# Units of 256 tokens of one batch instead of 128 tokens of two batches, with the state carried inside the unit

## The chip, the cores and the metric

One core of one Trainium2 chip runs the whole program. The metric is device time in microseconds (us). A kernel is run several times, beside runs of the kernel before on the same chip. Each run comes with the mean clock that was granted to TensorE, as a share of full speed. Runs marked slow are left out of every ratio. Stretches of a trace are counted from the start of the profiled execution. Its span is about 2 us shorter than the device time, so spans are compared with spans and times with times.

## The reference, cut to what matters

```python
# q, k, v, alpha: (batch 4, heads 8, tokens 768, width 48), float32
for t in range(S):                       # gated linear attention
    state = alpha[:, :, t, :, None] * state + einsum('bhd,bhe->bhde', k[:, :, t], v[:, :, t])
    y[:, :, t] = einsum('bhd,bhde->bhe', q[:, :, t], state)
x = y.transpose(0, 2, 1, 3).reshape(B * S, H * D)       # 3072 x 384
g = maximum(x @ w1, x @ w2)                              # 384 -> 1024
return g @ w_out                                         # 3072 x 384
```

Both kernels use max(a, b) = relu(a - b) + b. The hidden layer is relu(x (w1 - w2)), and the rest is x (w2 w_out), with w2 w_out computed once at the start. The recurrence is done in chunks of 128 tokens. A chunk needs the scores of its tokens (q k, masked), what they take from the state before it, and the new state, which is k v summed plus the old state times its decay.

## The kernel before

A unit is one chunk of 128 tokens of two batches, so its two halves are independent. There are 12 units. Unit u takes its state from unit u - 2, and units 0 and 1 take none. Loads go out on SP's queue and outputs on ScalarE's. All matmuls are float16.

```python
def load_alpha(u):                    # two halves, rows of two tokens (384 B)
    ...
    for bb in range(2):
        nc.sync.dma_start(out=t["af"][64 * bb : 64 * bb + 64], in_=alpha[...])
def load_kqv(u, bbs):                 # rows of one token (192 B), 128 partitions
    ...
    for name, src in (("kf", k), ("qf", q), ("vf", v)):
        nc.sync.dma_start(out=t[name][:, lo:hi]..., in_=src[2 * g + lo : 2 * g + hi, :, c * C : (c + 1) * C, :]...)
...
def state(u):                         # GpSimd: old state times decay, both batches at once
    if u >= NG:
        ...
        nc.gpsimd.tensor_mul(out=X["sb"], in0=st[u - NG]["tm"], in1=dd...)
...
for u in range(2, NU):                # the loop, cut
    pairs(u, 0)                       # scores (pp) of half 0, two masks (pt) on VectorE
    kv(u)                             # k v sums; VectorE adds sb -> tm
    ...                               # hidden groups 0, 1 of unit u - 1; decays, k, state of u + 1
    pairs(u, 1)
    hid(u - 1, 2); ystate(u); hid(u - 1, 3)
    ...; yin(u)                       # ya += masked scores times v
    outp(u - 1, 0); ...; xturn(u); ...; outp(u - 1, 1)   # ends with the store, on ScalarE's queue
    load(u + 4)
```

"Dummies" are matmuls on zeros that keep TensorE busy in the start-up while it waits.

## Time and profile before

| | before |
|---|---|
| time, 4 runs beside the changed kernel | 154.81 us median (154.14 to 155.47) |
| span of the profiled run, mean granted clock | 152.9 us, 0.997 |
| first hidden matmul of unit 0 | 25.36 us |
| hidden layer of unit 1 starts | 41.76 us |
| unit 2, unit 3, unit 11 start (first score matmuls) | 45.36, 53.51, 134.47 us |
| last output copy ends | 150.19 us |

These times come from the timeline of TensorE. In the groups of instructions, "idle before" is the idle time of an engine just before the instruction, with the instruction or transfer that ended it.

### The profile page before, as it was taken

What the parts mean: (1) busy time and instruction counts of PE and PEld (TensorE: products, weight loads), DVE (VectorE), ACT (ScalarE), POOL (GpSimd) and SP (SyncE); (2) the same over time, 40 slices, a digit from 0 to 9 for tenths busy, and PEclk for the clock granted to TensorE, in tenths of its full rate; (3) what the DMA queues carried; (4) which work ended last, traced back from release to release, by engine and by line L of the source; (5) the groups of instructions that cost most, each with busy time, mean ns of one, the idle gap of its engine ahead of it and who ended that gap; (6) DMA issues with size and microseconds to landing.
All of it is one profiled execution on the core that took longest, in us unless ns stands there. A gap on an engine that the chain in (4) does not pass through costs nothing.

```text
span 152.9 us, 4086 instructions
## 1 busy us (share of the span) xinstructions
PE 140.0 (92%) x1671; PEld 96.0 (63%) x1671; DVE 93.2 (61%) x192; ACT 78.5 (51%) x165; POOL 47.5 (31%) x73
## 2 busy tenths in 40 slices
PE   6878888787699999999999999999999999999991
PEld 2236454454386676777776777777767767767660
DVE  5057815676279596687685857876849565653010
ACT  3374136713566576194491861935818529244421
POOL 6032220340171816236072180450811705400000
PEclk9999999999999999999999999999999999999998
DMA  3999999999999999997999999999999992020202
GB/s 82 203 392 216 355 224 324 179 200 139 268 192 191 168 260 142 209 245 164 195 225 210 194 251 175 278 188 226 222 191 235 189 145 82 4 103 4 101 2 103
DMA packets 93459, 28.58 MB, mean 187 GB/s; under 512 B 87424, under 2 KB 93056, under 8 KB 93440
## 3 DMA queue, kind: packets, MB, share of 16 engines
q1 hardware_dynamic: 90160, 23.60, 88.3%
q10 hardware_dynamic: 3280, 4.72, 9.1%
q8 instruction: 13, 0.21, 0.7%
q14 instruction: 6, 0.05, 0.1%
HBM read 23.59 MB, written 4.72 MB: 185 GB/s over the span
## 4 chain that ended last, share of the span: by engine, by line
PE 65%; SPq 15%; DMA 9%; ACT 3%; DVE 2%; issue 1%; ACTq 1%; POOL 0%; DVEq 0%
PE op L370 19%; PE hp L352 17%; PE op L368 8%; SPq L80 7%; DMA qf<-in_q_dram 6%; PE tp L243 5%; SPq L103 4%; DMA vf<-in_v_dram 4%; PE pp L279 3%; PE cs L186 3%; PE ya L303 2%; PE kv L259 2%; SPq L68 2%; PE xp L318 2%; DVE pt L281 2%; PE ya L291 2%
## 5 line engine op out<-in xcount | busy, mean ns | idle before, releaser
L232 POOL TENSOR_TENSOR kn<-kf,Em 128x384 f16<-128x384 f32 x24 | 23.6, 1000 | 71.7 <-ACT Em L197 60.2
L352 PE MATMUL hp<-xt,w 128*128 128x256 f16 x288 | 37.6, 273 | 2.0 <-DVE w L409 1.2
L281 DVE TENSOR_TENSOR pt<-pp,u 128x512 f16<-128x512 f32 x48 | 30.9, 686 | 13.0 <-PE pp L279 12.6
L370 PE MATMUL op<-wo,gT 128*128 128x384 f16 x192 | 35.1, 326 | 0.0
L373 ACT COPY outs<-op 128x384 f32<-128x384 f32 x24 | 11.5, 478 | 41.9 <-PE op L370 41.9
L352 PEld LDWEIGHTS <-w 128*128 128x128 f16 x288 | 25.7, 98 | 7.7 <-DVE w L409 2.5
L370 PEld LDWEIGHTS <-gT 128*128 128x128 f16 x192 | 18.8, 98 | 12.4
L245 DVE COPY qk<-tp 128x1024 f16<-128x1024 f16 x24 | 16.5, 687 | 10.4 <-PE tp L243 10.3
L357 ACT ACTIVATE gT<-hp 128x512 f16<-128x512 f32 x36 | 20.4, 593 | 3.8 <-PE hp L352 3.6
L236 DVE TENSOR_TENSOR qn<-qf,cs 128x384 f16<-128x384 f32 x24 | 12.3, 548 | 9.6 <-ACT de L207 6.4
L160 ACT ACTIVATE lg<-af 128x768 f16<-128x768 f32 x12 | 10.1, 843 | 11.7 <-DMA af<-in_alpha_dram 7.5
L368 PE MATMUL op<-w2o,xt 128*128 128x384 f16 x72 | 15.6, 325 | 0.0
L359 DVE TENSOR_SCALAR gT<-hp 128x512 f16<-128x512 f32 x12 | 8.3, 691 | 8.3 <-PE hp L352 8.3
L416 PE MATMUL warm<-wz 128*128 128x512 f16 x39 | 12.2, 439 | 1.3 <-DVE halves L123 1.3
L197 ACT ACTIVATE Em<-cs 128x384 f32<-128x384 f32 x24 | 11.7, 488 | 1.1 <-PE cs L186 1.1
L169 POOL CAST v<-vf 128x768 f16<-128x768 f32 (+1 forms) x14 | 10.2, 730 | 6.1 <-DMA vf<-in_v_dram 6.1
L202 ACT ACTIVATE cs<-cs 128x384 f32<-128x384 f32 x24 | 11.8, 492 | 0.0
L267 DVE TENSOR_TENSOR tm<-kv,sb 64x192 f32<-64x192 f32 x32 | 11.3, 353 | 0.5
L243 PE MATMUL tp<-ident,qn 128*128 128x128 f16 x96 | 9.3, 219 | 1.2 <-DVE qn L236 1.2
L279 PEld LDWEIGHTS <-qk 48*128 48x128 f16 x192 | 6.2, 94 | 6.1 <-issue 3.4
L243 PE MATMUL tp<-ident,kn 128*128 128x128 f16 x96 | 9.3, 219 | 0.4 <-POOL kn L232 0.4
L279 PE MATMUL pp<-qk 48*128 48x128 f16 x192 | 9.5, 217 | 0.2 <-DVE qk L245 0.2
(57 smaller groups left out, 142.6 us busy)
## 6 DMA issues: line engine op xcount, KB each, us to landing
af<-in_alpha_dram SPq DMA_DIRECT2D x24, 192.0 KB, 5.5
out_dram<-outs ACTq DMA_DIRECT2D x11, 384.0 KB, 4.0
kf<-in_k_dram SPq DMA_DIRECT2D x10, 384.0 KB, 6.0
qf<-in_q_dram SPq DMA_DIRECT2D x10, 384.0 KB, 7.6
vf<-in_v_dram SPq DMA_DIRECT2D x10, 384.0 KB, 7.0
w2f<-in_moe_w_dram SPq DMA_DIRECT2D x3, 512.0 KB, 5.1
wof<-in_moe_w_out_dram SPq DMA_DIRECT2D x2, 768.0 KB, 7.4
w1f<-in_moe_w_dram SPq DMA_DIRECT2D x4, 384.0 KB, 8.7
```

The source lines that it names most:

```text
L202: nc.scalar.activation(out=X["csv"][bb], in_=X["csv"][bb], func=ACTF.Exp)
L232: nc.gpsimd.tensor_mul(out=X["kn"][bb][:, :, 0:D], in0=X["kf"][:, bb], in1=X["Em"][bb])
L236: nc.vector.tensor_mul(out=X["qn"][bb][:, :, 0:D], in0=X["qf"][:, bb], in1=X["csv"][bb])
L243: nc.tensor.transpose(tp[:, n, j, :], pair(src, j), ident)
L245: nc.vector.tensor_copy(out=qk, in_=tp)
L279: nc.tensor.matmul(pa[a][:, j, :], lhsT=qk[r, 1, j, :], rhs=qk[r, 0, j, :], start=True, stop=True)
L281: nc.vector.tensor_mul(out=pt[:, a], in0=pa[a], in1=u16.unsqueeze(1).to_broadcast([128, HP, C]))
L352: nc.tensor.matmul(hp[:, n, :], lhsT=w12[:, ds, f * 128 : (f + 1) * 128], rhs=X["xt"][:, ds].rearrange("p n t -> p (n t)"), start=(ds == 0 ...
L357: nc.scalar.activation(out=gT[:, 2 * f2 : 2 * f2 + 2, :], in_=hp, func=ACTF.Relu)
L368: nc.tensor.matmul(op, lhsT=X["xt"][:, ds, n, :], rhs=w2o[:, ds, :], start=(ds == 0), stop=False)
L370: nc.tensor.matmul(op, lhsT=X["gT"][:, f, n * C : (n + 1) * C], rhs=wo16[:, f, :], start=False, stop=(f == NF - 1))
L416: nc.tensor.matmul(warm, lhsT=wz[:, 0:128], rhs=wz, start=True, stop=True)
```

## The change

The intent is wider rows. Within one batch, alpha and v of 256 tokens can be loaded as 128 partitions of two tokens each. That gives one transfer for each, with rows of 384 B instead of 192 B for v. k and q are brought into the same (parity, pair) order by two transfers for each half. The price is that the second half of a unit now needs the state of its first half, in every unit from the first on.

```diff
+    def load_fat(u, name, src):                 # alpha and v: one transfer, 384 B rows
+        nc.sync.dma_start(out=t[name].rearrange("p h j d -> p h (j d)"),
+                          in_=rows(src, u, 0, 2 * C).rearrange("h (p j) d -> p h (j d)", j=2))
+    def load_rows(u, name, src, cc):            # k and q: two transfers of 64 partitions
+        for j in range(2):
+            nc.sync.dma_start(out=t[name][64 * j : 64 * j + 64, cc],
+                              in_=rows(src, u, cc * C, C).rearrange("h (p j) d -> j p h d", j=2)[j])
...
-    def state(u):                               # once a unit, from unit u - 2
+    def state(u, cc):                           # once a half
+        if cc: tm, de0 = X["tm0"], X["de"][:, :, 0, 0]           # from the first half
+        else:  tm, de0 = st[u - B]["tm1"], st[u - B]["de"][:, :, 1, 0]
...
-        nc.gpsimd.tensor_copy(out=X["v16"][:, e], in_=X["vf"][:, e])
+        for cc, j in ((0, 0), (1, 1), (0, 1), (1, 0)):           # v casts: GpSimd and ScalarE
...
-            nc.scalar.dma_start(out=dst, in_=X["outs"])
+            nc.sync.dma_start(out=dst[j], in_=X["outs"][r])       # for j in 0, 1: halves, on SP
...
     for u in range(2, NU):
-        pairs(u, 0)
-        kv(u)
+        if u + 4 < NU:
+            load(u + 4)
+        pmm(u, 0); kvmm(u, 0); pmask(u, 0); kvsum(u, 0)
+        state(u, 1)
+        if more(u): kvmm(u, 1)
```

The start-up is reordered to match: both weight products and the whole of unit 0's attention come before its first hidden matmul.

## The prediction

> **What bounds the kernel now.** I read the page's engine table and its 40 slices first.
>
> ```profile
> PE 140.0 (92%) x1671; PEld 96.0 (63%) x1671; DVE 93.2 (61%) x192; ACT 78.5 (51%) x165; POOL 47.5 (31%) x73
> ...
> PE   6878888787699999999999999999999999999991
> ...
> DMA  3999999999999999997999999999999992020202
> ```
>
> TensorE has gaps only in the first 12 slices (46 us). The DMA row is just as full up to slice 33, so the next question is which of the two sets the pace. The table by stretches of 10 us answers it.
>
> ```profile
> 0.00:10.00 10.00, 7.35 (x41) 2.96 (x42) 2.81 (x25) 4.35 (x8) 3.89 (x15) 1.00 0.88 203
> 10.00:20.00 10.00, 8.69 (x95) 4.98 (x93) 7.80 (x15) 4.19 (x6) 2.33 (x3) 1.00 1.15 293
> 20.00:30.00 10.00, 8.20 (x65) 4.76 (x63) 4.60 (x6) 6.29 (x13) 1.83 (x2) 1.00 1.12 245
> 30.00:40.00 10.00, 7.77 (x86) 4.53 (x84) 6.62 (x14) 2.46 (x5) 2.00 (x3) 1.00 1.16 194
> 40.00:50.00 10.00, 9.16 (x129) 6.73 (x127) 7.08 (x14) 6.56 (x15) 4.47 (x6) 1.00 1.26 204
> ...
> 80.00:90.00 10.00, 10.00 (x137) 7.42 (x136) 7.17 (x15) 5.73 (x14) 3.67 (x6) 1.00 1.26 215
> ```
>
> The first number after the width is TensorE's busy time. Of its 12.9 idle us (152.9 - 140.0), 8.8 lie before 50 us; afterwards TensorE is solid. So there are two stages. The **prologue** (weights, units 0 to 2) ends at 53.5 us, where unit 3's first score matmuls start. The **steady loop** follows; the chain that ended last, read in order of time, is TensorE alone there:
>
> ```profile
> 84.12 0.33 PE pp L279 x8
> 84.45 0.45 PE kv L259 x8
> 84.90 1.31 PE hp L352 x12
> ...
> 92.94 1.30 PE op L370 x8
> 94.24 0.33 PE pp L279 x8
> ```
>
> One unit takes 94.24 - 84.12 = 10.12 us, all matmuls. From 53.5 to the end are 99.4 us that no transfer can shorten.
>
> The prologue, in the timeline, is paced by weights: w1 lands in quarters, VectorE subtracts, TensorE follows.
>
> ```profile
> 24.34 1.99 DVE L409 TENSOR_TENSOR w<-w1f,w2f 128x768 f16<-128x768 f32 x2 [2.18 <-DMA w1f<-in_moe_w_dram]
> ...
> 25.36 0.83 PE L352 MATMUL hp<-xt,w 128*128 128x256 f16 x6 [0.32 <-DVE w L409]
> ```
>
> **What the Trainium skill says.** "DMA: Bandwidth & Descriptors", section Specifications, puts the least size for line rate at 512 B. The trace agrees: by windows of 1 us, stretches of 192 B rows run at 180 to 210 GB/s, alpha's 384 B rows at 280 to 330, w2's 4 KB rows at 406 to 414. Its section Rules for kernel authors says that two transfers to disjoint partition halves serialize and are better joined. The change joins alpha's halves but splits every k and q transfer into halves; no run shows yet what that costs. "GPSIMD Engine Reference", section 4.1, calls GpSimd about 2x slower on two-input work; kn takes 1000 ns there, qn of the same shape 548 ns on VectorE. "TensorE: Matmul & The Clock Gate", section Back-to-back issue gap, gives N/2.4 + 2.5 ns when warm: 162.5 ns for 384 columns. The chain's 8 in 1.30 us are 162.5: no slack inside.
>
> **The change, part by part.**
>
> *Transfers.* Before, each unit loads 1024 rows of 384 B (alpha) and 6144 of 192 B; after, 2048 of 384 B (alpha, v) and 4096 of 192 B. At 190 and 310 GB/s: 1.18 MB/190 + 0.39/310 = 7.5 us before, 0.79/190 + 0.79/310 = 6.7 after: 0.8 us less a unit. In the prologue w2 no longer waits for v of unit 0, so weights land about 0.8 to 1 us earlier. Issues per unit go from 5 to 10 at 0.6 us each, 6 us, below the 6.7: hidden. In the loop the gain is worth nothing, as TensorE needs 10.1.
>
> *Matmuls.* Counts match over the program (80 kv matmuls, 160 state reads), one dummy less. Unit 3 has 8 fewer state reads: -0.15 us.
>
> *The prologue's order.* Before, units 0 and 1 need no state; the two batches run separately. Now their second half needs the first half's state: kv matmuls, VectorE kvsum (2 x 0.356), GpSimd sb (half of the old 0.83: 0.5), then the state read. The built program also shows output copies before the second wo cast on ScalarE, and the xt copy before all four w1-w2 subtractions on VectorE. I place them with measured durations:
>
> - w2 casts end at 12.2; third w2T copy 15.1; q multiply 15.65; transposes 16.1; qk copy 16.85; kvsum(0,0) 17.55; sb 18.05; GpSimd's wo cast 18.9; first weight product 18.95 to 21.05; state read and pt.v 21.65; two xn copies (0.43 each) 22.45; second wo cast 23.3 (before: 22.1); second product 25.35; six transposes 25.7; xt copy (0.55) 26.3; first subtraction 27.3.
> - So the first hidden matmul starts at **27.3 instead of 25.36**, and w1's earlier landing is worth nothing. The four subtractions in a row (1.0 each) end at 30.2, the fourth hidden group at 30.95 (before 29.5).
> - Unit 1: op(0,0) to 32.7; transposes 33.15; qk 33.9; pp 34.3; two masks (0.645 each) 35.65; q multiply 36.2; transposes 36.5; op(0,1) 38.25; masks of the second half 39.9; kvsum 40.65; sb 41.2; second kvsum 42.0, which also frees the PSUM buffer that the state read takes; read and pt.v 42.7; xn 43.45; transposes 43.85; xt 44.45. Unit 1's hidden layer starts at **44.5 instead of 41.76**.
> - ScalarE then has Exp of unit 2 (four x 0.49 and 0.19) to 45.65 and its new half of the v casts (2 x 0.45) to 46.55, before the first Relu at 47.15, which frees the PSUM buffer for the third hidden group. That ends at 47.85, transposes 48.3, fourth group 48.95. Unit 2 starts at **48.95 instead of 45.36**.
> - Unit 2: VectorE does Relu to 49.7, masks 51.0, kvsum 51.7, waits for sb to 52.25, kvsum 53.0, masks 54.3; pt.v ends 54.5; op 56.3; turns 57.55. Unit 3 starts at **57.55 instead of 53.5: +4.0 us**.
>
> *The loop.* In a unit, after its start: masks to 1.66, kvsum 2.4, sb 2.97, second kvsum 3.76, masks 5.05. TensorE wants the state's PSUM buffer at 3.74 and the last mask at about 5.1. It just fits; I book 0.1 us of waiting for each of units 3 to 7 (+0.5), none from 8 on, where the second kvsum is gone. A unit before lost 0.35 to the late q of unit 4, which landed at 60.33 and lands earlier now (-0.35). ScalarE's two v casts, 0.9 us, fit the 2.5 us that it idles between output copies. Output goes by the SP queue in two halves: hidden, except the last, perhaps -0.1.
>
> *Sum:* +4.0 + 0.5 - 0.35 - 0.15 - 0.1 = +3.9, so 158.7. My chain has no gap in it that a wait I overlooked could fill, but several that earlier data could shorten; I set 158.3.
>
> **Rivals.**
> - *The transfers set the prologue* and its whole length shrinks with rows: 2.4 us by the end of unit 2's load. The DMA row speaks for it. Against it: in the new order xt, not w1, is last before the subtractions. It would give 152.5 to 154.
> - *A tuned order hides the state chain.* The dummy matmuls (39 x about 0.21 us apart, 8 us) are padding, so TensorE has room; if two of my joints overlap better, +2 remains: 156.5 to 157.5.
> - *Halved transfers starve the loop.* If SP's 10 loads and 2 stores took over 10 us a unit (0.85 each; now 0.57 to 0.8 where nothing blocks), units would stretch: 162 or more. Against it: the free issues of today.
> - *The in-unit state chain binds every unit.* If GpSimd's small products cost 0.8 instead of 0.5, TensorE waits 0.4 in five units: 160.
>
> **Range and chances.** The loop is sure to about 1 us, the prologue to about 2. Range 155.8 to 161.0. The 2% lines are 151.7 and 157.9. Faster needs the first rival in full: 0.03. My centre is barely above 157.9: slower 0.57, same 0.40.
>
> **What would show it.** In the profile after: unit 0's first hidden matmul near 27.3 with VectorE's subtractions as its releaser and no DMA wait before them; unit 1's hidden layer near 44.5; unit 3's first pp near 57.5; units then 10.1 to 10.2 apart with TensorE waiting under 0.1 us at the state reads; sb near 500 ns; about 78700 packets on the load queue instead of 90160 (73728 rows, 2944 of weights, 16 for each of 129 transfers). I am wrong if unit 3 starts before 55, if the steady unit exceeds 10.4, or if kf or qf transfers stand among the long waits after 60 us.

## The result

| | before | after |
|---|---|---|
| time, 4 runs each | 154.81 us median (154.14 to 155.47) | 161.03 us median (160.70 to 161.59) |
| ratio | | 1.0406, 95% interval 1.0352 to 1.0459 |
| span, mean granted clock | 152.9 us, 0.997 | 158.9 us, 0.989 |
| first hidden matmul of unit 0 | 25.36 | 27.59 |
| hidden layer of unit 1 | 41.76 | 46.43 |
| unit 2, 3, 11 start | 45.36, 53.51, 134.47 | 50.33, 59.03, 139.87 |
| last output copy ends, then to the end | 150.19, 2.74 | 155.46, 3.43 |

A ratio is worked out from the fast runs of both kernels, so it is not quite the ratio of the medians. The kernel became 6.2 us slower, where the prediction had 3.5 us. The times of the four runs do not follow their clocks: 160.70 came at a mean clock of 0.989, 160.96 at 1.000. So what follows about the clock holds for the profiled run first.

The engine table and the 40 slices of the changed kernel, to set beside those of before:

```profile
PE 141.4 (89%) x1670; PEld 97.6 (61%) x1670; DVE 92.3 (58%) x190; ACT 92.4 (58%) x189; POOL 53.6 (34%) x104
...
PE   6978667958679798999999999999999999999990
PEclk9999999995999999999999999999999999999999
DMA  4999999896999799698999979799896903021113
```

TensorE is again solid from slice 17 on, so the loop is not where the time went. The PEclk row has something that before did not have: a 5 in the tenth slice (35.8 to 39.7 us). TensorE's busy time rose by 1.4 us with one instruction fewer. Stretches of 2 us show it better (after the width: busy time and count of PE, PEld, DVE, ACT and POOL, then granted clock, DMA share, GB/s):

```profile
32.00:34.00 2.00, 1.26 (x13) 0.82 (x11) 0.69 (x1) 1.10 (x3) 1.24 (x3) 1.00 1.30 255
34.00:36.00 2.00, 0.73 (x12) 0.45 (x12) 1.52 (x3) 0.39 (x1) 0.23 (x2) 0.96 1.40 176
36.00:38.00 2.00, 1.72 (x9) 1.05 (x10) 0.92 (x2) 0.00 (x0) 0.00 (x0) 0.50 0.43 77
38.00:40.00 2.00, 2.00 (x14) 0.94 (x14) 0.00 (x0) 0.06 (x1) 0.00 (x0) 0.69 0.83 162
```

TensorE works 2.0 of the 4 us up to 36. After that it is granted half its clock for 3.4 us, just when an output product of 11 matmuls runs. The timeline has that product:

```profile
36.28 0.61 PE L267 MATMUL tp<-ident,qn 128*128 128x128 f16 x4 [1.51 <-DVE qn L260]
36.68 1.17 PE L383 MATMUL op<-w2o,xt 128*128 128x384 f16 x3
37.64 2.26 PE L385 MATMUL op<-wo,gT 128*128 128x384 f16 x8
```

In the chain of waits these 11 matmuls take 3.0 us (0.96 + 2.05). At full clock in the loop they take 1.79 (0.49 + 1.30).

In the loop the chain of waits shows the new path inside a unit (start, duration, what; here unit 3, which started at 59.03):

```profile
59.95 1.28 DVE pt L309 x2
...
61.49 0.37 DVE tm L291
...
62.03 0.49 POOL sb L252
...
62.90 0.37 DVE tm L289
63.27 0.04 issue
63.31 0.26 PE ya L327 x7
```

Masks, k v sum, GpSimd's state product and second sum stand in a row, and TensorE waits for the last one. In unit 2 and unit 3 this costs time: unit 3 takes 10.62 us (before 10.43). From unit 4 on a unit takes 10.14, and from unit 8 on 9.88. The eight units from the start of unit 3 to that of unit 11 take 80.84 us, against 80.96 before.

So the 5.96 us of span divide as follows: start-up to unit 3 +5.52, units 3 to 10 -0.12, unit 11 to the last copy -0.13, the last stores +0.69.

### The profile page after: what moved, and what is told of

It is laid out like the page before. It is cut to its first block, busy times and chain, and to the rows that moved or that the text cites. A ratio compares the mean times of both kernels' runs of the same rounds, so it can differ in the third digit from the quotient of the medians.

```text
span 158.9 us, 4250 instructions
## 1 busy us (share of the span) xinstructions
PE 141.4 (89%) x1670; PEld 97.6 (61%) x1670; DVE 92.3 (58%) x190; ACT 92.4 (58%) x189; POOL 53.6 (34%) x104
## 4 chain that ended last, share of the span: by engine, by line
PE 67%; SPq 13%; DVE 9%; DMA 3%; ACT 3%; issue 3%; POOL 1%; POOLq 0%; DVEq 0%
PE op L385 19%; PE hp L367 19%; PE op L383 8%; PE tp L267 6%; SPq L82 4%; SPq L118 4%; PE pp L303 3%; DVE pt L309 3%; DMA kf<-in_k_dram 3%; PE ya L339 3%; SPq L72 2%; PE ya L327 2%; PE cs L212 2%; PE xp L354 2%; PE kv L276 2%
## 5 line engine op out<-in xcount | busy, mean ns | idle before, releaser
L309 DVE TENSOR_TENSOR pt<-pp,um 128x512 f16<-128x512 f32 x48 | 30.9, 685 | 14.6 <-PE pp L303 14.4
L385 PE MATMUL op<-wo,gT 128*128 128x384 f16 x192 | 35.9, 331 | 0.0
L252 POOL TENSOR_TENSOR sb<-tm,dd 128x192 f16<-128x192 f32 x20 | 10.1, 506 | 59.7 <-DVE tm L289 36.7
L372 ACT ACTIVATE gT<-hp 128x512 f16<-128x512 f32 x36 | 21.5, 599 | 5.7 <-PE hp L367 4.8
L383 PE MATMUL op<-w2o,xt 128*128 128x384 f16 x72 | 16.1, 333 | 0.0
L346 ACT CAST xn<-ya 128x384 f16<-128x384 f32 x24 | 10.4, 481 | 8.1 <-PE ya L339 7.8
L196 ACT CAST v<-vf 64x384 f16<-64x384 f32 x24 | 12.2, 510 | 3.0 <-DMA vf<-in_v_dram 2.5
L194 POOL CAST v<-vf 64x384 f16<-64x384 f32 x24 | 12.0, 501 | 2.8 <-DMA vf<-in_v_dram 2.1
L356 DVE COPY xt<-xp 128x768 f16<-128x768 f16 x12 | 6.6, 550 | 10.3 <-PE xp L354 10.3
L183 ACT ACTIVATE lg<-af 128x768 f16<-128x768 f32 x12 | 10.1, 844 | 3.0 <-DMA af<-in_alpha_dram 2.7
```

Source lines behind the costliest of these rows:

```text
L194: nc.gpsimd.tensor_copy(out=o, in_=i)
L196: nc.scalar.copy(out=o, in_=i)
L309: nc.vector.tensor_mul(out=pt[:, a], in0=X["pa", cc][a], in1=um.unsqueeze(1).to_broadcast([128, HP, C]))
L372: nc.scalar.activation(out=gT[:, 2 * f2 : 2 * f2 + 2, :], in_=hp, func=ACTF.Relu)
L383: nc.tensor.matmul(op, lhsT=X["xt"][:, ds, n, :], rhs=w2o[:, ds, :], start=(ds == 0), stop=False)
L385: nc.tensor.matmul(op, lhsT=X["gT"][:, f, n * C : (n + 1) * C], rhs=wo16[:, f, :], start=False, stop=(f == NF - 1))
```

## The experiments

The theory had four terms: (1) the new order and the state chain in the start-up, as predicted; (2) the clock dip; (3) the halved k and q transfers; (4) the last stores, now in halves. The rival to (2) is that the dip is a by-product and the order alone costs 5.5. Short diffs are against the changed kernel unless another is named.

### e1_warm: fill two waits in the start-up with dummies

> The changed kernel with 9 more dummy matmuls in unit 1's waits (3 after its first transposes, 6 after its first score matmuls), nothing else. Theory: between 32 and 36.3 us TensorE was busy for under half of the time, and then worked 36 to 40 us at a granted clock of 0.50 to 0.69; op(0,1) took 3.0 us where warm ones take 1.79. With the gaps filled, the clock stays at 1.00, op(0,1) takes 1.8 us, and unit 3 starts about 1.3 us earlier: 159.7 us. Rival, the clock dip only fills time in which unit 2's transfers or VectorE would have been waited for: below 0.4 us gained, 160.6 or more.

```diff
     turn(1, 0)
+    dummies(3)
     kmul(1, 1)
     pairs(1, 0)
+    dummies(6)
```

It took 161.76 us (ratio 1.0419, 1.0373 to 1.0466): a miss. The clock stayed at 1.00 from 34 to 44, as intended, but TensorE was busy only 0.83 of the 2 us from 42 to 44, and the clock fell to 0.80, 0.50 and 0.85 from 44 to 50. First hidden matmuls also came late in this profile (28.72, as w_out landed over 1 us later). The dip had moved, so its worth was not measured.

### e2_cast_first: the second w_out cast ahead of the output copies on ScalarE

> The changed kernel with one line moved: on ScalarE the second cast of wo stands before the two output copies of unit 0, not after them. Theory (order, not transfers, delays the first hidden layer): wo's second half landed at 20.4 us, so the cast ends near 21.3 instead of 23.4, the second weight product starts near 21.9 instead of 23.5, the first hidden matmul near 26.0 instead of 27.59, and about 1.2 to 1.6 us of that reaches the end: 159.5 us. Rival, transfers pace the start: VectorE then waits for w1 quarters and the first hidden layer moves by under 0.5 us: 160.6 or more.

```diff
     wmul(0)
+    wcast(1)
     ystate(0)
     yin(0)
-    wcast(1)
```

The first hidden matmuls came at 26.64 instead of 27.59, but the median was 161.87. Its profile is of a run marked slow, with two dips (35 to 38.5 and 55.6 to 59 us), and three of its four runs were marked slow. The one fast run took 159.24.

One pair of profiles would not be enough here. Nine profiles (the changed kernel, e1, e3, e7, e10, e11, e12, e14, e15) have the same start-up up to this point (e3 and e11 clear one more tile), and in them the first hidden matmul comes anywhere from 27.05 to 28.80. What moves it is the landing of the first half of w_out, which the first wo cast waits for (here in the changed kernel):

```profile
18.22 0.83 ACT L422 CAST wo<-wof 128x768 f16<-128x768 f32 x1 [1.08 <-DMA wof<-in_moe_w_out_dram]
...
21.86 0.86 ACT L346 CAST xn<-ya 128x384 f16<-128x384 f32 x2 [2.81 <-PE ya L339]
...
22.60 0.84 ACT L422 CAST wo<-wof 128x768 f16<-128x768 f32 x1
```

From the start of that cast to the first hidden matmul are 9.37 us in all nine, and 7.95 in e2, whose clock is 1.00 up to there. So the place of the second cast behind the output copies (22.60, though its data had landed at 20.37) was worth 1.4 us of the start-up. What of that reaches the end, the times do not tell.

### e3_no_chain: the second half takes its state from zeros

> Wrong result on purpose: the second half's state is made from a tile of zeros instead of the first half's sum, so GpSimd's product no longer waits for VectorE; every instruction stays. Theory: the state chain inside the unit costs about 0.7 us each in units 1, 2 and 3 and 0.1 in units 4 to 7, and nothing in unit 0 (the weight product is later there): 2.0 to 2.4 us in all, 158.8 us. If the in-unit chain were the whole cause of the 6 us, it would come near 155; if it is nothing but order and clock, it stays above 160.4.

```diff
-            tm, de0 = X["tm0"], X["de"][:, :, 0, 0]
+            tm, de0 = zt, X["de"][:, :, 0, 0]       # zeros: a wrong result on purpose
```

The result is wrong (relative error 0.125). In the trace unit 2 takes 8.14 us instead of 8.70, unit 3 10.05 instead of 10.62, and units of the loop 10.05 instead of 10.14. Unit 1 gained as well: its start-up had no dip in this run, and from the first hidden matmul to unit 1's hidden layer are 16.77 us, against 17.41 in e7 below, which has the chain and no dip either. That makes 0.65, 0.56, 0.57 and four times 0.09 us, 2.1 in all, as expected piece by piece. Yet the median was 162.75 us (ratio 1.0461, 1.0397 to 1.0526). In the profiled run (161.37) two things hid the gain: w_out landed 1.2 us later than in the changed kernel's profile, and a new wait appeared, with 13.1 us for unit 5. The chain of waits, in order of time:

```profile
75.79 3.76 DMA out_dram<-outs
...
79.65 0.48 ACT outs L391
...
80.15 0.51 ACT v L196
...
81.25 0.34 PE kv L279 x4
```

ScalarE's output copy waits for an output store to land, since there are two output buffers. Behind that copy stand ScalarE's casts of v, and behind these TensorE's k v matmuls. Before the change neither the casts nor the stores were placed so.

### e4_one_transfer: k and q of a half unit as one transfer of 128 partitions

> Wrong result on purpose: k and q of a half unit come in one transfer of 128 partitions in plain row order instead of two of 64 partitions, the same bytes and rows of 192 B; 6 transfers a unit instead of 10. Theory: the transfers are not what paces the changed kernel; the time stays within 0.5 us of 161.0, and the loop's unit at 10.1 us. Rival, the doubled number of issues delays the start: 2 us or more are gained, 159 or less.

```diff
-        for j in range(2):
-            nc.sync.dma_start(out=t[name][64 * j : 64 * j + 64, cc], in_=...[j])
+        nc.sync.dma_start(out=t[name][:, cc], in_=rows(src, u, cc * C, C).rearrange("h p d -> p h d"))
```

The token order is then wrong, and so is the result. The rows keep their 192 B, but they are now neighbours in memory, where the changed kernel's transfers take every second row. So the edit changes two things, and they were not told apart. It took 159.92 us (ratio 1.0284, 1.0242 to 1.0325), against a ratio of 1.0406 for the changed kernel beside its own runs of before. The third w2 cast of ScalarE, in the timelines of before, of the changed kernel and of this one:

```profile
12.23 1.04 ACT L431 CAST w2h<-w2f 128x1024 f16<-128x1024 f32 x1 [0.37 <-DMA w2f<-in_moe_w_dram]
```

```profile
12.60 1.04 ACT L446 CAST w2h<-w2f 128x1024 f16<-128x1024 f32 x1 [1.13 <-DMA w2f<-in_moe_w_dram]
```

```profile
10.87 1.04 ACT L444 CAST w2h<-w2f 128x1024 f16<-128x1024 f32 x1 [0.40 <-DMA w2f<-in_moe_w_dram]
```

With whole transfers the weights do land earlier than before, by 1.4 us, where the prediction had 0.8 to 1. With halves this cast starts at 11.86 to 12.69 in the nine profiles, around the 12.23 of before, so nothing is gained. The first half of w_out lands at 17.23, and at 17.66 to 19.41 in the nine. Against the one profile of the changed kernel the first hidden matmul moves from 27.59 to 26.70 and unit 3 from 59.03 to 58.26, with the clock dip still there, which gives the halves 0.8 us. That the ratio moves by 1.2% (about 1.9 us) may come from w_out landing later in most runs than in that profile; it was not traced.

### e5_tail: the kernel before, with its last two stores in halves on ScalarE and SP

> The kernel before, with the last unit's two outputs each sent as two transfers of 64 partitions, one from ScalarE's queue and one from SP's, as the changed kernel does. Theory: the changed kernel's end, from the last output copy to the end of the span, is 3.4 us instead of 2.7 because of these halves, so this kernel is 0.4 to 0.8 us slower than the one before (155.5 against 155.0). Rival, that end is long for another reason (rows two tokens apart): no change, under 0.2 us.

```diff
-            nc.scalar.dma_start(out=dst[:, n], in_=X["outs"][:, n])
+            nc.scalar.dma_start(out=dst[0:64, n], in_=X["outs"][0:64, n])
+            nc.sync.dma_start(out=dst[64:128, n], in_=X["outs"][64:128, n])
```

155.75 us, ratio 1.0025 (0.9988 to 1.0063), so the times alone do not decide. In the traces the span from the end of the last copy grows from 2.74 to 3.45 us, the same 0.7 as in the changed kernel (3.43). Halves land in 2.2 to 2.5 us, the whole tile in 1.9.

### e6_halves: the kernel before, with each k, q and v transfer cut into two halves

> The kernel before, with each k, q and v transfer cut into two of 64 partitions: the same bytes and rows, 8 transfers a unit instead of 5. The run with k and q in one transfer each was 1.2% nearer to the kernel before than the changed kernel is, with its first hidden layer about 1 us earlier. Theory (more issues and halves delay the weights, and the first hidden layer there is paced by w1): 1.5 to 2.5 us slower than before, its first hidden matmul near 27 instead of 25.4. Rival, halves cost nothing in themselves: within 0.5 us of before.

```diff
-            nc.sync.dma_start(out=t[name][:, lo:hi]..., in_=src[..., c * C : (c + 1) * C, :]...)
+            for r in (0, 64):
+                nc.sync.dma_start(out=t[name][r : r + 64, lo:hi]..., in_=src[..., c * C + r : c * C + r + 64, :]...)
```

162.80 us, ratio 1.0428 (1.0352 to 1.0504). This was not the clean measure it was meant to be. The first 10 us move 154 GB/s instead of 203 and the first hidden matmul comes at 26.93 instead of 25.36. But after that SP's loads wait 8.1 us for output stores on the other queue, and there is a clock dip of 6.8 us. It only shows that cutting transfers is not free at the start.

### e7_warm_more: 18 dummies in the waits of unit 1

> The changed kernel with 18 more dummy matmuls in all, in every wait of unit 1 (3 and 6 as in the first run of that kind, 5 before unit 1's state read, 1 and 3 around its turn). The first run removed the dip at 36 to 40 us and got one at 40 to 50 us instead, with no gain. Theory: without any dip the prologue from the first hidden matmul to unit 3's first score matmuls takes near 30.0 us instead of 31.4, the mean granted clock of the span is 0.997, and the time is 1.0 to 1.5 us below the changed kernel's, 159.8. Rival, the dips hide in other waits: 161 or more.

```diff
 (as e1_warm, and)
     sums(2)
+    dummies(5)
     ystate(1)
...
-    dummies(3)
+    dummies(4)
     xturn(1)
+    dummies(3)
```

The clock stayed at 1.00 in all windows of the start-up, here where the changed kernel had 0.96 and 0.50:

```profile
34.00:36.00 2.00, 1.97 (x18) 0.98 (x18) 1.62 (x3) 0.30 (x1) 0.27 (x2) 1.00 1.24 158
36.00:38.00 2.00, 1.81 (x14) 1.22 (x15) 0.82 (x2) 0.00 (x0) 0.00 (x0) 1.00 0.45 78
```

From the first hidden matmul (27.49) to unit 3 (57.51) are 30.0 us, instead of 31.4 with the dip; e10 below has the same 30.0. The predicted unit 3 was 57.55. This decides against the rival that the order alone costs 5.5: without the dip it costs 4.0 (57.51 - 53.51). A dip does not always cost as much: 30.6 us in e14 and 31.0 in e1, where it falls later. The gain did not reach the end: 161.04 us (ratio 1.0334, 1.0268 to 1.0399; fast runs from 159.78 to 161.79), and the profiled run of 161.79 has a unit of 12.7 us in the loop. The timeline shows the store that causes it:

```profile
68.24 0.48 ACT L388 COPY outs<-op 128x384 f32<-128x384 f32 x1 [1.47 <-PE op L385]
...
74.06 1.30 SPq L396 DMA_DIRECT2D out_dram<-outs  x2
...
79.81 0.48 ACT L388 COPY outs<-op 128x384 f32<-128x384 f32 x1 [5.55 <-DMA out_dram<-outs]
```

The output tile is complete at 68.7, and its store is issued at 74.06, after the loads that stand ahead of it in SP's program. The next copy into that buffer waits until 79.8. In the kernel before, ScalarE issues the store right after the copy (copy ends 64.52, issue 64.55). SP is busy issuing for 9.1 to 9.5 us of a unit's 10.1. It was so before, too (9.3 to 9.9), but no store stood in its queue then.

### e8_combined: several repairs of the start-up at once

> The changed kernel put right where the theory says that it loses, correct result: q of the first half issued from ScalarE's queue, the second wo cast before the output copies, unit 1 ordered so that its multiplies, transposes and state chain overlap its output product, half of the v casts of unit 2 after the Relus, dummies in the waits, and a third output buffer. Theory: unit 2 starts near 45 instead of 50.3 and unit 3 near 53.3 instead of 59.0, and the rest takes 99.5 as before: 155 us, within 1 us of the kernel before. Rival, SP's 10 loads and 2 stores a unit are then the pace, as in the run without the chain, where a unit of 13.1 us waited for an output store: 158 or more, with ScalarE waiting for output transfers.

```diff
-                nc.sync.dma_start(out=t[name][64 * j ...])
+                (nc.scalar if u == 0 and cc == 0 and name == 'qf' else nc.sync).dma_start(...)
-    X["outs"] = mp.tile(..., tag="outs", bufs=2)
+    X["outs"] = mp.tile(..., tag="outs", bufs=3)
+    wcast(1)  before ystate(0); unit 1 reordered; v casts of unit 2 split around its Relus; 4 + 2 dummies moved or added;
+    ScalarE's preload of its function table moved behind the first loads
```

Correct, 156.27 us, ratio 1.0042 (0.9985 to 1.01). First hidden matmul 25.24, unit 3 at 54.26, no long unit in the loop. A dip stayed (0.80, 0.50, 0.85 from 36 to 42), after TensorE was busy 1.30 and 1.39 of 2 us. As it joins many edits, it says what can be had, not which edit gives it.

### Four runs together: e9_fill, e10_three_out, e11_chain_three, e12_store_act

> The combined kernel (156.27; its profile shows TensorE busy 1.30 and 1.39 of 2 us between 34 and 38 and a granted clock of 0.80, 0.50, 0.85 from 36 to 42, and unit 3 starting at 54.26) with three dummy matmuls ahead of unit 1's first kv matmuls and three after its second scores. Theory that the clock falls after windows in which TensorE is idle about a third of the time: no dip at 36 to 42, unit 3 starts at 52.8 to 53.5 and the median is 154.8 to 155.5, level with before. Rival that the clock dips somewhere in most runs whatever is filled: another dip later, 156 again.

> The changed kernel with the 18 extra dummies (161.04; its profile had unit 3 at 57.51 and then a unit of 12.7 us) and a third buffer for the output tile, nothing else. Theory that an output store stuck in SP's queue behind loads holds one of two output buffers and so stalls ScalarE's output copy: no unit over 10.7 us, unit 3 at 57.5, median 159.3 to 159.9. Rival that the stall comes from the loads themselves (v or k late): the stall stays, 160.5 to 161.5.

> The kernel whose second half takes no state of the first (162.75, wrong result on purpose, with one unit of 13.1 us) and a third output buffer. Theory: the stall goes, and what stays is the worth of the state chain: unit 3 at 57.5 without a clock dip, every unit from 3 on 10.05 or 9.9, median 159.3 to 160.0; the chain is then worth about 1.5 of the 6.2 us. Rival that the stall has another cause: 162 or more again.

> The changed kernel with the 18 extra dummies and two output buffers as it has, but with the output stores issued on ScalarE's queue, as before the change. If the stall comes from the stores' place in SP's queue behind loads, it goes, units stay 10.0 to 10.15, median 159.3 to 160. If the 8 completion semaphores that loads and stores share in turn are what holds, SP's loads wait for stores instead and the stall may move to v or k transfers: 160.5 or more.

```diff
 e9_fill (against e8_combined)
     outp(0, 1)
+    dummies(3)
     kvmm(1, 0)
...
     pmask(1, 1)
+    dummies(3)
 e10_three_out (against e7_warm_more), e11_chain_three (against e3_no_chain)
-    tag="outs", bufs=2
+    tag="outs", bufs=3
 e12_store_act (against e7_warm_more)
-                nc.sync.dma_start(out=dst[j], in_=X["outs"][r])
+                nc.scalar.dma_start(out=dst[j], in_=X["outs"][r])
```

**e9_fill**: 155.29 us, ratio 1.0021 (0.9958 to 1.0083), level with before, and unit 3 at 53.11. Its stretches from 36 on, where e8 had 0.80 and 0.50:

```profile
36.00:38.00 2.00, 1.46 (x15) 0.59 (x15) 1.44 (x4) 1.07 (x3) 0.16 (x2) 1.00 0.79 144
38.00:40.00 2.00, 1.80 (x35) 1.14 (x35) 0.00 (x0) 1.57 (x5) 0.98 (x1) 1.00 0.89 189
```

**e10_three_out**: 159.83 us (158.83 to 159.94), ratio 1.0299 (1.0247 to 1.0352). Nothing in the loop takes over 10.62 us, and ScalarE's copies wait for no store any more. This is what the theory said; by the times alone e10 is not apart from e7, as the intervals overlap.

**e11_chain_three**: 158.14 us, ratio 1.0212 (1.0146 to 1.0277). The stall is gone, though the profiled run has a clock dip. Unit 2 takes 8.14, unit 3 10.05. It came out a little faster than the 159.3 to 160.0 expected. It differs from e3 in the third buffer alone, and the intervals lie apart (1.0397 to 1.0526 there): here the buffer is shown to be worth over 2%.

**e12_store_act**: 170.79 us, ratio 1.0978 (1.0887 to 1.107), far above what was expected of the theory and well into the open end of the rival ("160.5 or more"). The long unit of e7 is gone, but from unit 4 on units take 10.9. The chain of waits inside unit 5:

```profile
80.87 0.49 ACT outs L388
...
81.38 0.63 ACTq L396
...
82.05 0.62 ACTq L396
...
82.72 0.84 ACT lg L183
```

ScalarE issues the two halves itself, 1.25 us, and only then takes the logarithm that the next unit's sums wait for. In the kernel before one whole store took 0.38 us to issue. Besides, SP's loads waited 24.1 us in all for output stores: in the trace the transfers of both queues signal their ends on the same eight semaphores (counters by which engines learn of an end) in turn. The two effects were not told apart. So the old queue would not have been a cheaper place for halved stores in this kernel as it is.

### The last three, for what was still open: e13_kv_first, e14_after_three, e15_after_again

> The filled kernel (155.29 on its chip, before 155.44) with the order inside each unit from unit 2 on changed: kv matmuls ahead of the scores, and VectorE's kv sums ahead of the two masks, so that GpSimd's state product runs while VectorE masks. The kernel without the chain had units 2 and 3 at 8.14 and 10.05 instead of 8.70 and 10.62, and units 4 to 7 at 10.05 instead of 10.15. If that is only VectorE's wait for GpSimd, this order hides it: units 2 and 3 at 8.1 to 8.3 and 10.05 to 10.2, median 154.0 to 154.6. If the later scores push the masks and the pt.v matmuls back by as much, 155.3 stays.

> The changed kernel with three output buffers and nothing else. Its four runs lay at 160.70 to 161.59, and the one with a granted clock of 1.0 took 160.96, so a clock dip is not all that its runs have beyond the predicted order. If some of its runs have the output store's stall, this is 0.5 to 1.0 faster than the control run beside it: about 160.2. If not, the two agree within 0.3.

> The changed kernel again, unchanged, as the control: 160.7 to 161.6, spread over runs with a clock dip (mean granted clock under 0.99), with an output stall (a unit of over 11 us) or with neither (about 159.7).

```diff
 e13_kv_first (against e9_fill)
-        pmm(u, 0); kvmm(u, 0); pmask(u, 0); kvsum(u, 0); state(u, 1)
+        kvmm(u, 0); pmm(u, 0); kvsum(u, 0); state(u, 1); pmask(u, 0)
 e14_after_three (against the changed kernel)
-    tag="outs", bufs=2
+    tag="outs", bufs=3
 e15_after_again: the changed kernel, no edit
```

**e13_kv_first**: 154.70 us (154.09 to 155.04), ratio 0.9989 (0.9952 to 1.0025). Unit 2 takes 8.29, unit 3 10.27, and the next four 10.05. In the chain the state product is no longer a piece:

```profile
53.75 0.36 DVE tm L292
...
54.14 1.30 DVE pt L310 x2
...
56.62 0.20 PE ya L328 x8
```

VectorE sums first and masks next, so that GpSimd's product runs beside the masks. The chain is thus a wait that an order can mostly hide, not a shift of all that follows. This is the lowest median of all the changed forms. Its interval includes 1, so it is level with before and not shown to be faster; it also overlaps that of e9, so the gain over e9 rests on the unit times.

**e14_after_three** and **e15_after_again**, with e10, stand on one chip beside the same runs of before. The means of their fast runs are 161.65 us for e15 (six runs), 160.41 for e14 (four), 159.61 for e10 (four). By these means a third output buffer alone takes 1.2 us off, and the 18 dummies another 0.8. The intervals of e15 (1.0386 to 1.0479) and e14 (1.0283 to 1.0419) overlap, and those of e14 and e10 (1.0247 to 1.0352) do too, so neither step is shown by itself; that of e10 lies below e15's entirely, so both together are. e14 and e11 differ in nothing but the state chain (and a tile of zeros), and their intervals lie apart: 160.41 against a mean of 158.25, so the chain is worth about 2.2 us, as the 2.1 of the traces said. e15's profile fell in a slow run, so no trace of the unchanged kernel shows a stall in the loop. What points to it is e15's run of 161.95 at a granted clock of 0.997, which is long although it had hardly a dip. A late landing of w_out, which moves the start by up to 1.75 us from run to run, would do as well.

One more reading of e14 belongs here, since it limits what was said of the dip. Its profile has a stretch as thin as any before a dip, and the clock did not fall there at once:

```profile
34.00:36.00 2.00, 0.49 (x9) 0.32 (x8) 1.69 (x3) 1.02 (x2) 1.20 (x3) 1.00 1.41 207
36.00:38.00 2.00, 2.00 (x20) 1.10 (x19) 0.69 (x1) 0.03 (x1) 0.00 (x0) 1.00 0.82 113
...
42.00:44.00 2.00, 2.00 (x22) 1.13 (x22) 0.00 (x0) 1.35 (x4) 0.02 (x1) 0.50 1.31 248
```

It fell after the next one (0.66 of 2 us from 40 to 42). Thin stretches came before the dips that were looked at closely, and filling them took the dips away in e7, e9 and e10, but a thin stretch does not always bring one.

The clock records of the traces say more. In the changed kernel the clock first rises at 5.11, falls at 35.83 and rises again at 39.25; in e14 the times are 3.90, 41.44 and 44.86. All dips before the end of the work last 3.41 us or twice that, and begin a whole number of 3.41 us after the first rise (9 and 11 in these two). So the busy time has to be summed over stretches on that grid. In the changed kernel TensorE was busy 1.56 of the 3.41 us up to 35.83. In e14 the same gap of 1.51 us lies across two stretches, with 2.25 and 2.29, and the clock stayed; the next had 2.07, and it fell. Over all 17 profiles every stretch busy for under 45% was followed by a dip and none over 70% was; between them it went either way, so this gives no sharp limit.

## Why the prediction was right or wrong, point by point

The direction was right, the size was not: +3.5 was recorded and +6.2 came, just over the top of the range. Two terms of the sum failed in the profiled run: the clock in the start-up (1.4 us) and the last stores (0.8 us).

- **First hidden matmul at 27.3**: measured 27.59, with VectorE's subtraction as the releaser and no DMA wait before it. The order was right, and e2 confirms that the second cast stood in the path (9.37 us down to 7.95). That the number fits so well is in part luck, since nine profiles of this start-up spread from 27.05 to 28.80 with the landing of w_out.
- **Unit 1's hidden layer at 44.5, unit 2 at 48.95, unit 3 at 57.55**: measured 46.43, 50.33, 59.03. From the first hidden matmul to unit 1's hidden layer were 17.2 predicted and 18.84 measured. Without a dip they are 17.4 (e7 and e10). So the order was sized right up to there; from there to unit 2 it had 4.45 and 3.90 came, so that unit 3 in e7 (57.51) fits its 57.55 better than the pieces do. **The step that failed is that every matmul in the start-up was costed at full clock**: "op(0,1) to 38.25" had 1.75 us and took 3.0. The prediction's own list has TensorE idle from 33.15 to 33.9 and from 34.3 to 36.2, and did not ask what this does to the clock. That is 1.4 us of the profiled run (31.44 against 30.02). Over the runs it is less sure: e14 to e10 gives 0.8, not shown by itself.
- **Weights land 0.8 to 1 us earlier; 10 issues "hidden"**: wrong. The third w2 cast started at 12.60 (11.86 to 12.69 in the nine profiles) instead of 12.23. The halved transfers ahead of w2 took the gain away (e4: 10.87 with whole ones in plain order). Since xt was last before the subtractions, as said, part of it stayed hidden: 0.8 us at unit 3.
- **The loop: +0.5, -0.35, -0.15**: 0.0 as a sum, and -0.12 measured, by luck. Unit 3 was to gain 0.4 and lost 0.19, as the chain costs it 0.57 and not 0.1; units 8 to 10 gained 0.56 where nothing was booked. sb costs 506 ns, as predicted, and the steady unit 10.14. None of the signs of being wrong came true: unit 3 started after 55, no steady unit went over 10.4, and no load of k or q held up TensorE after 60 us. (One idle time of GpSimd, 5.2 us before sb, is put down to a load of k; it is as long in units where VectorE's sum ends it.)
- **Output "hidden, except the last, perhaps -0.1"**: both parts failed. The last stores cost +0.69 (e5: +0.71 in the kernel before). And the others are not always hidden: in SP's in-order queue they stand behind loads, and with two buffers ScalarE's copy can wait for them (e3 and e7 show it, e10 removes it). In the profiled run of the changed kernel copies waited 3.9 us for stores, without holding TensorE up. Over its runs this may be 1.2 us (e14 against e15), which is not shown.
- **Rivals**: the start-up did not shrink with wider rows, and w1 was not waited for. But its begin is set by a transfer all the same, the landing of w_out, which the prediction did not place. The rival of halved transfers that starve the loop was near in its mechanism and wrong in its form: SP's 9.1 to 9.5 us of issues do not stretch a unit, but can keep a store waiting. The in-unit chain binds units 1 to 3 (0.65, 0.56, 0.57) and hardly the four after (0.09). Hiding it needed an order that the change does not have (e13).
- **A slip in a reading**: the gaps of TensorE's row before end with slice 11 (42 us), not 12. Nothing rests on it.

The sum closes on one chip. e10, with neither dips nor stalls, is 4.4 us over before by medians (159.83 - 155.44). The prediction's +3.9, with the measured +0.7 for the last stores in place of -0.1, gives 4.7. Between the means of e10 and e15 lie the other 2.0 us. The dummies and the third buffer together take them off, so they are put down to the two terms that the prediction did not have, clock and waiting stores. Open is how they divide in a usual run of the unchanged kernel, and what decides about the clock between 45% and 70%.

## What to carry to other kernels

Where a change makes TensorE wait longer in several short waits, price the work after them at the lower clock too, and look at the granted clock in narrow stretches before calling the order the cause. Before an output store is moved onto the queue that issues the loads, look at what stands ahead of it in that queue and count the output buffers; the third buffer was the cheap repair here (e3 to e11). Before one profile is set beside another, check with several runs of the same start-up how far its transfers move by themselves. In a chain of two engines, start the other engine's piece before the work that does not depend on it.

## What the Trainium skill lacked or had wrong

- "TensorE: Matmul & The Clock Gate", section HAM oscillation, gives the rule of no idle gaps over about 3.4 us, and section What's actually happening lets the clock fall after at least one idle window of that length. Here the longest single gap ahead of the dip was 1.51 us, TensorE was busy 1.56 of the 3.41 us before it, and the clock fell to 0.50. Its section A second HAM failure mode tells of short idles that make the clock swing, but no section says what share of busy time holds it: in 17 profiles under 45% never did and over 70% always did.
- "DMA: Bandwidth & Descriptors", Rules for kernel authors, says that two transfers to disjoint halves serialize and that one is better. The runs agree that one is better, and give the size that it lacks: the halved k and q transfers, with their rows two tokens apart, cost 1.2% here (e4), and halved last stores 0.7 us in the trace (e5).
- The same table says that spreading transfers over queues only saves issue time of the sequencer. Here the other side of that counted: moving two halved stores to ScalarE's queue put 1.25 us of issues on its path, in a kernel that went to 170.79 us (e12). That a store behind loads in one queue holds its buffer (issued 5.3 us after its data was ready, a unit of 12.7 us) was found on none of the pages read.
